# Row maxima turned by VectorE and DRAM, and stationary sides kept for a second matmul, in a transformer block on one core

## The chip, the cores and the metric

One Trainium2 chip, one of its cores. The kernel is written directly against the engines: TensorE (matmuls, PE in the profile, its weight loads PEld), VectorE (DVE), ScalarE (ACT), GpSimd (POOL) and SyncE (SP), whose queue issues nearly all DMAs. The metric is the device time of one execution in microseconds, median of several runs.

## What is computed

A block with 2048 rows of width 512: layer norm with modulation from a condition vector, attention with 32 query heads of 16 and one shared key and value head, a residual, a second modulated norm, and a gated FFN of width 1792 with another residual.

```python
mod = (_silu(c) @ w_mod).reshape(c.shape[0], 6, 1, -1)
h = _layernorm(x) * (1 + ca) + sa
q = (h @ wq) split into 32 heads of 16;  k = h @ wk;  v = h @ wv
p = softmax(q k^T * 16 ** -0.5)
x = x + ga * ((p @ v) heads joined @ wo)
h = _layernorm(x) * (1 + cb) + sb
x = x + gb * ((sigmoid(h @ w_gate) * (h @ w_up)) @ w_down)
```

The weights are scaled up, so scores are large, and the softmax needs its row maxima.

## The kernel before

Numbers are kept as pairs of fp16 (high and low part), and a product of two pairs is three matmuls: high by high, high by low, low by high (`term` gives the stationary and the moving side of the n-th of them).

**Units.** Queries are cut into 8 blocks of 256 rows and the heads into 4 groups of 8, so there are 32 units (`units`). For a unit, `qp` holds on each row half of TensorE (partitions 0 to 63 and 64 to 127) the queries of four heads: high, low and high part in 48 rows, then two rows (48 and 49) that hold minus-signed parts of the row maxima, so that a score tile comes out of the matmul with its maximum subtracted. `kp` holds the keys in the same layout.

**Two passes over the scores.** The first gives the maxima: `a_product` multiplies 128 queries of one head (stationary) with 512 keys (moving) into a bank `sa` (a ring of three), and `a_max` has VectorE reduce it to one column of `mx`. `spot(n)` tells which head, query tile and key quarter is the n-th of a unit's 64 tiles. This pass runs 84 tiles ahead (`A0`). The second pass, `st_tile`, multiplies 128 keys (stationary) with 512 query columns (moving) into a bank `st` (a ring of two), and ScalarE takes the Exp into `P`. `pv` multiplies V by `P` into the bank `craw`, in fp32, which makes two passes of each matmul.

**How maxima become rows.** When a unit's 64 tiles are done, `max_end` reduces `mx` over the key quarters (two reductions on VectorE). A step later `max_rows` has TensorE transpose the result with an identity into a bank of the `sa` ring; ScalarE scales it and rounds it to fp16; `low` has VectorE take the low part, and four DMAs on SP write the rows into `qp`.

**Small tiles.** In the main loop every product of 128 stationary columns is issued by `columns` as four matmuls of 64 rows by 32 columns, each with a weight load of its own. Products on different row halves stream at the same time.

**The main loop.** Each unit has 16 steps, each step two rounds. The order within a round is written out in `ORDER`: a0, s0, c, a1, s1 stand for the two `sa` tiles, the two `st` tiles and `pv`. The `sa` and `st` tiles of a round use one row half, `pv` the other; `sides` swaps the halves every two steps. After each round `piece` issues some terms of the projections and the FFN (the groups `pq`, `po`, `pgu`, `pd`), which a planner (`pace`, `parts`, `plan`) spreads evenly over the rounds to come; a `Couple` runs two such groups side by side, one on each row half, and swaps them at half time. `part(n0, n1)` issues the terms n0 to n1 of a couple. `piece` also calls `drip`, which issues one FFN transpose or weight load on SP. Most other follow-up work is put off by a number of steps (`defer`), so that it finds its inputs ready.

Ahead of the main loop, `PLAN` lists token by token what is issued for the first norm, the projections and the first 84 `sa` tiles. After it a tail finishes the last block with matmuls on the whole array.

Of the kernel before, what the change touches and what calls it, by code (L numbers as in the profile page):

```python
# [8 lines left out]
F16 = mybir.dt.float16  # L9
# [41 lines left out]
)  # L51
# [4 lines left out]
A0 = 84  # L56
ORDER = "a0", "s0", "c", "a1", "s1"
LAG = 2
# [38 lines left out]
def adaln_mqa_glu_kernel(  # L97
# [53 lines left out]

    def columns(dst, l_, r_, start, stop):
        for c_ in range(0, P, 32):
            pe.matmul(dst[c_:c_ + 32], l_[:, c_:c_ + 32], r_, start=start, stop=stop)

# [42 lines left out]
    class Couple:  # L198
# [3 lines left out]
        def part(self, n0, n1):  # L202
            if n0 == 0:
                for g in self.gs:
                    g.open()
            m = self.gs[0].n
            for n in range(n0, n1):
                if n == m:
                    assert self.since is not None or done[0] > self.marks
                    take_over(self.since)  # L210
                for j in (1 - side[0], side[0]):
                    g = self.gs[j ^ (n >= m)]
                    l_, r_, *cut = g.term(n % m, slice(64 * j, 64 * j + 64))
                    columns(cut[0](g.bank) if cut else g.bank, l_, r_, n == 0, n == 2 * m - 1)
                if n == m - 1:
                    self.since, self.marks = None, done[0]
                    if open_[0]:
                        hand_over()
                        self.since = done[0]
                if n in self.after:  # L220
                    self.after[n]()
            if n1 == self.n:
                for k, g in enumerate(self.gs):
                    g.end(g.bank, k == 1)
# [367 lines left out]

    def spot(n):
        return n // 16, n // 8 % 2, n % 2, n // 2 % 4

    def a_product(i, n):
# [3 lines left out]
        kc, qt, j, r = spot(n)  # L600
        sa = sbank("sa")
        l_, r_ = qp[64 * j:64 * j + 64, r, qt * P:(qt + 1) * P], kp[64 * j:64 * j + 64, kc * 512:(kc + 1) * 512]
        if first:
            pe.matmul(sa, l_, r_, start=True, stop=True)
        else:
            columns(sa, l_, r_, True, True)
        return i, n, sa

    def a_max(i, n, sa):
        kc, qt, j, r = spot(n)  # L610
# [5 lines left out]
    def a_tile(i, n):  # L616
        a_max(*a_product(i, n))

    pend, seen = [], {}

    def max_end(i):
        m16 = wp.tile([64, 32], F32, tag="m16", name="m16", bufs=4)
        for u in range(2):
            dve.tensor_reduce(m16.rearrange("p (h t u) -> p h t u", t=2, u=2)[:, :, :, u], mxs[i][64 * u:64 * u + 64],
                              axis=AX.X, op=ALU.max)
        return lambda: max_rows(i, m16)

    def max_rows(i, m16):
        qp = get_q(i)
        pm = sbank("sa")  # L630
        pe.matmul(pm[:32, :64], m16, ident[:64, :64], start=True, stop=True)
        m32 = wp.tile([32, 64], F32, tag="m32", name="m32", bufs=4)
        act.activation(m32, pm[:32, :64], AF.Identity, scale=1.0 / SM)
        mh = wp.tile([32, 2, 64], F16, tag="mh", name="mh", bufs=4)
        act.activation(mh[:, 0], m32, AF.Identity)

        def low():
            dve.tensor_tensor(mh[:, 1], m32, mh[:, 0], op=ALU.subtract)
            for h in range(2):
                for j in range(2):  # L640
                    r = 64 * j + 48 + h
                    sp1.dma_start(qp[r:r + 1], mh[16 * j:16 * j + 16, h, :])

        return low

# [193 lines left out]
    def ffn_block(b, end_of_all=False):  # L839
# [63 lines left out]
        def gu_pair(p, t, m):  # L903
# [4 lines left out]
            def term(n, rs):  # L908
                k, i = divmod(n, 3)
                h_, w_ = ((0, 0), (1, 0), (0, 1))[i]  # L910
                return h2[t][0][rs, 4 * h_ + k, :], gws[at + NDC * p + k][rs, 2 * w_ + m]
# [12 lines left out]
        def gu_last(t):  # L924
# [5 lines left out]
            def term(n, rs):  # L930
                k, i = divmod(n, 3)
                gw = gws[at + NDC * NPR + k // 2].rearrange("p m n -> p (m n)")
                h_, w_ = ((0, 0), (1, 0), (0, 1))[i]
                c0 = (2 * (k % 2) + w_) * 512
# [145 lines left out]
    def q_end(b, o):  # L1080
# [8 lines left out]
              "pm": mod_product, "me": mod_copy, "pr": mod_sum, "m": mod_end,  # L1089
              "a": a_next, "x": lambda: a_max(*held.pop(0)), "mx": lambda: rows.append(max_end(0)), "my": lambda: rows.append(rows.pop()()), "mz": lambda: rows.pop()(),  # L1090
              "lw": load_wq, "lx": load_x, "lm": lambda i: load_mod(i, sp1), "bl": lambda: blanks.append(blank(pool1)), "lq": load_q}
# [103 lines left out]
    vq = []  # L1195
    lows = []

    for i, (b, o) in enumerate(units):
# [5 lines left out]
        for kb in range(NKB):  # L1204
# [5 lines left out]
            for z in [z for z in waits if z[0] <= s]:  # L1210
                waits.remove(z)
                z[1]()
            ready_rows, rows[:] = rows[:], [max_end(*z) for z in late]
            an = A0 + 4 * (s - kb % 2)
# [3 lines left out]
            for n in range(2):  # L1218
                t = kb - kb % 2 + n
                for z in ORDER:  # L1220
                    k = int(z[1:] or 0)
                    if z[0] == "a" and an + 4 * n + 2 * k + 1 - h < len(alist):
                        a_tile(*alist[an + 4 * n + 2 * k + 1 - h])
                    if z == "c" and vq:
                        pv(*vq[n], second)
                    if z[0] == "s":
                        st_tile(i, t, k, 1 - h, second)
                if n == 0:
                    lows[:] = [z() for z in ready_rows]
                piece(s, n)  # L1230
                if n == 1:
                    for z in lows:
                        z()
            if second:
# [70 lines left out]
```

## Time and profile before

| | us |
|---|---|
| median of 3 runs | 1639.52 (1636.52 to 1640.59) |
| the profiled execution | 1629.06 |
| its span | 1627.3 |
| TensorE busy | 1585.3 (97%) |
| VectorE busy | 1417.1 (87%) |
| ScalarE busy | 1288.7 (79%) |
| first score tile of the main loop starts at | 105.1 |

A group's row gives line, engine, operation, output<-inputs, shapes and count, then busy time, mean ns of one, then the idle time before its instructions and what ended it. A timeline row gives start, length (both us), engine, line, operation and count. Nearly all instructions carry line 143, a helper that keeps the written order, so groups are told apart by the names of their tiles. Busy time of TensorE is the union of matmuls that overlap; what it could still take shows in their starts.

### The profile page before, as it was taken

The page shows a single profiled execution, that of the slowest core. Times are in us where ns is not written, and L with a number is a line of the kernel's source. Part 1 is how long each engine was busy: PE and PEld are TensorE (multiplying, and loading weights), DVE is VectorE, ACT ScalarE, POOL GpSimd, SP SyncE. Part 2 cuts the span into 40 slices and gives each one's busy share as a digit, 9 for nine tenths or more (in the row PEclk, how much of TensorE's full clock was granted, in tenths as well). Part 3 has the DMA queues.
Part 4 walks back from the last instruction along what each step waited for, and adds up shares of the span by engine and source line. Part 5 has one row for each costly group of instructions (what it writes and reads, how often), then busy time and mean ns, then how long its engine had stood idle before and what let it go on. Part 6 is the DMA issues. An engine that isn't in the chain of part 4 may idle for free.

```text
span 1627.3 us, 91846 instructions
## 1 busy us (share of the span) xinstructions
PE 1585.3 (97%) x41481; PEld 987.3 (61%) x41481; DVE 1417.1 (87%) x2400; ACT 1288.7 (79%) x2325; POOL 666.2 (41%) x827
## 2 busy tenths in 40 slices
PE   6899999999999999999999999999999999999998
PEld 3335554546666666666666666666666666665465
DVE  7789999999999999999999999999999999993041
ACT  4539998888888888888888888888888888888600
POOL 5453877244425332443226232543226322533223
PEclk9979999999999999999999999999999999999999
DMA  7122554044521233114321433115411343124411
GB/s 238 71 84 65 164 156 131 28 118 106 139 68 29 75 97 108 31 39 130 92 63 33 89 85 106 30 38 128 112 42 42 81 121 85 23 60 107 116 65 52
DMA packets 185076, 140.22 MB, mean 86 GB/s; under 512 B 96372, under 2 KB 144492, under 8 KB 184684
## 3 DMA queue, kind: packets, MB, share of 16 engines
q1 hardware_dynamic: 184684, 134.34, 30.4%
q8 instruction: 325, 5.32, 1.3%
q14 instruction: 67, 0.55, 0.1%
HBM read 97.18 MB, written 16.24 MB: 70 GB/s over the span
## 4 chain that ended last, share of the span: by engine, by line
PE 88%; DVE 4%; ACT 2%; DMA 2%; POOL 1%; issue 1%; SPq 1%; POOLq 0%; ACTq 0%; DVEq 0%
PE craw L143 24%; PE sa L143 18%; PE pgu L143 17%; PE st L143 11%; PE pd L143 8%; PE po L143 2%; PE pgu L194 2%; PE pq L143 2%; PE pd L194 2%; DVE mx L143 2%; ACT th L143 1%; DMA lc<-lD 1%; SPq L143 1%; DMA xall<-in_A_x_dram 1%; ACT P L143 1%
## 5 line engine op out<-in xcount | busy, mean ns | idle before, releaser
L143 DVE TENSOR_REDUCE mx<-sa 128x1 f32<-128x512 f32 x2048 | 1299.8, 683 | 69.6 <-PE sa L143 33.2
L143 ACT ACTIVATE P<-st 128x512 f32<-128x512 f32 x2048 | 1179.3, 598 | 204.7 <-PE st L143 143.7
L143 PE MATMUL craw<-P,V 64*32 64x512 f32 x8192 | 1086.0, 597 | 1.0 <-ACT cs L143 1.0
L143 PE MATMUL st<-qp,kp 64*32 64x512 f16 x8192 | 832.7, 379 | 7.3 <-ACT P L143 6.1
L143 PE MATMUL sa<-kp,qp 64*32 64x512 f16 (+1 forms) x7940 | 827.9, 378 | 8.2 <-DVE mx L143 6.2
L143 PEld LDWEIGHTS <-kp 64*32 64x32 f16 x8192 | 323.1, 91 | 249.2 <-issue 79.1
L143 PE MATMUL pgu<-gw,h 64*32 64x512 f16 x9408 | 407.4, 376 | 3.2 <-DMA gw<-wD 1.2
L143 PEld LDWEIGHTS <-qp 64*32 64x32 f16 (+1 forms) x7940 | 270.2, 92 | 149.1 <-issue 58.7
L143 PEld LDWEIGHTS <-h 64*32 64x32 f16 (+1 forms) x9600 | 212.7, 92 | 77.8 <-issue 22.6
L143 PEld LDWEIGHTS craw<-P,V 64*32 64x32 f32 x8192 | 184.4, 105 | 21.7 <-issue 2.6
L143 PE MATMUL pd<-wdh,g 64*32 64x512 f16 x2688 | 136.1, 376 | 0.7
L952 POOL TENSOR_SCALAR th<-th 128x512 f32<-128x512 f32 x49 | 30.2, 617 | 246.4 <-ACT th L143 223.2
L569 POOL MEMSET qp<- 32x1024 f16 x60 | 56.7, 944 | 118.6 <-PE st L143 100.5
L143 PEld LDWEIGHTS <-g 64*32 64x32 f16 x4032 | 82.0, 92 | 31.0 <-issue 6.5
L725 POOL TENSOR_TENSOR raw<-raw 128x256 f32<-128x256 f32 x31 | 22.7, 733 | 160.6 <-DMA raw<-lD 151.7
L143 PE MATMUL pd<-wdl,g 64*32 64x512 f16 x1344 | 80.5, 376 | 0.0
L953 POOL TENSOR_TENSOR th<-th,u 128x512 f32<-128x512 f32 x49 | 62.8, 1282 | 4.1
L1009 POOL TENSOR_TENSOR ot<-ot,gb 128x512 f32<-128x512 f32 x12 | 15.4, 1281 | 114.3 <-ACT ot L143 114.3
L143 DVE COPY u<-pgu 128x512 f32<-128x512 f32 (+1 forms) x49 | 31.6, 644 | 34.9 <-PE pgu L143 34.8
L143 PE MATMUL craw<-nought 64*32 64x1 f16 x357 | 58.2, 163 | 1.1 <-issue 1.1
L956 POOL TENSOR_TENSOR gr<-th,gr 128x512 f16<-128x512 f32 x49 | 57.1, 1165 | 4.1
L143 PE MATMUL pq<-h,wdh 64*32 64x512 f16 (+1 forms) x688 | 54.4, 390 | 0.1
(156 smaller groups left out, 1112.5 us busy)
## 6 DMA issues: line engine op xcount, KB each, us to landing
gw<-wD SPq DMA_DIRECT2D x224, 256.0 KB
wD<-gw SPq DMA_DIRECT2D x28, 256.0 KB
wm<-in_w_mod_dram SPq DMA_DIRECT2D x6, 1024.0 KB
qp<-qD SPq DMA_DIRECT2D x192, 32.0 KB
qD<-q SPq DMA_DIRECT2D x16, 256.0 KB
xr<-in_A_x_dram SPq DMA_DIRECT2D x16, 256.0 KB
out_dram<-ot SPq DMA_DIRECT2D x16, 256.0 KB
raw<-cs SPq DMA_DIRECT2D x248, 16.0 KB
```

What stands on the lines that cost most here:

```text
L143: return (lambda *a, **k: keep(f_(*a, **k))) if pinned else f_
L194: pe.matmul(cut[0](self.bank) if cut else self.bank, l_, r_, start=(n == 0), stop=(n == self.n - 1))
L569: eng.memset(qp[j:j + 32], 0.0)
L725: keep(pool.tensor_tensor(raw[:, :QU], raw[:, :QU], raw[:, QU:], op=ALU.mult))
L952: pool.tensor_scalar(th, th, 1.0, 1.0, op0=ALU.add, op1=ALU.mult)
L953: pool.tensor_tensor(th, th, u_, op=ALU.mult)
L956: pool.tensor_tensor(rows[:, 1], th, rows[:, 0], op=ALU.subtract)
L1009: pool.tensor_tensor(ot, ot, mods[5], op=ALU.mult)
```

## The change

Three things are changed together.

- **The maxima's way into `qp`.** `max_end` now makes one reduction over all 128 partitions and has ScalarE round its scaled result to fp16; `max_turn` has VectorE take the low part into the same tile of 32 columns and transpose that tile in blocks of 32 by 32; `max_down` writes it to DRAM in one DMA, and `max_rows` reads it back with two DMAs, each for both rows of one row half. The four parts follow one another round by round (`rows`), after the round's `piece`. TensorE has no part in it any more, and no bank of the `sa` ring.
- **Stationary sides kept.** `columns` gets `held`: with it, the four matmuls are issued without weight loads and use what the array still holds. `part` does so for the second of three terms (n % 3 == 1) unless it is the first of its piece; in `gu_pair` and `gu_last` the order of the terms is changed so that the second shares its stationary side with the first (elsewhere it did already).
- **Order of the maxima tiles.** For all units but the first, `spot` now pairs tiles: the two `sa` tiles of a round have the same head and query tile, and two neighbouring key quarters, so the second is issued as `held`. So that no other load on that row half falls between, `ORDER` becomes s0, a0, c, a1, s1.

```diff
-ORDER = "a0", "s0", "c", "a1", "s1"
+ORDER = "s0", "a0", "c", "a1", "s1"
...
-    def columns(dst, l_, r_, start, stop):
+    def columns(dst, l_, r_, start, stop, held=None):
         for c_ in range(0, P, 32):
-            pe.matmul(dst[c_:c_ + 32], l_[:, c_:c_ + 32], r_, start=start, stop=stop)
+            if held is None:
+                pe.matmul(dst[c_:c_ + 32], l_[:, c_:c_ + 32], r_, start=start, stop=stop)
+            else:
+                pe.add_instruction(mybir.InstMatmult(
+                    start_tensor_calc=start, stop_tensor_calc=stop, tile_size=(64, 32), tile_position=(held, c_), ldweights=False,
...
-                    columns(cut[0](g.bank) if cut else g.bank, l_, r_, n == 0, n == 2 * m - 1)
+                    columns(cut[0](g.bank) if cut else g.bank, l_, r_, n == 0, n == 2 * m - 1, 64 * j if n % 3 == 1 and n > n0 else None)
...
-    def spot(n):
-        return n // 16, n // 8 % 2, n % 2, n // 2 % 4
+    def spot(i, n):
+        if i == 0:
+            return n // 16, n // 8 % 2, n % 2, n // 2 % 4
+        return n // 32 * 2 + n // 2 % 2, n // 16 % 2, n % 2, n // 4 % 4
...
-            columns(sa, l_, r_, True, True)
+            columns(sa, l_, r_, True, True, 64 * j if held else None)
...
     def max_end(i):
-        m16 = wp.tile([64, 32], F32, tag="m16", name="m16", bufs=4)
-        for u in range(2):
-            dve.tensor_reduce(m16.rearrange("p (h t u) -> p h t u", t=2, u=2)[:, :, :, u], mxs[i][64 * u:64 * u + 64],
-                              axis=AX.X, op=ALU.max)
-        return lambda: max_rows(i, m16)
+        m = wp.tile([P, 16], F32, tag="m", name="m", bufs=2)
+        mm = wp.tile([P, 32], F16, tag="mm", name="mm", bufs=2)
+        dve.tensor_reduce(m, mxs[i].rearrange("p r t k -> p (r t) k"), axis=AX.X, op=ALU.max)
+        act.activation(mm[:, :16], m, AF.Identity, scale=1.0 / SM)
+        return lambda: max_turn(i, m, mm)
+
+    def max_turn(i, m, mm):
+        mt = wp.tile([P, 32], F16, tag="mt", name="mt", bufs=2)
+        mD = dr.tile([32, P], F16, tag="mD", name="mD", bufs=3)
+        dve.scalar_tensor_tensor(mm[:, 16:], m, 1.0 / SM, mm[:, :16], op0=ALU.mult, op1=ALU.subtract)
+        dve.transpose(mt, mm)
+        return lambda: max_down(i, mt, mD)
+
+    def max_down(i, mt, mD):
+        sp1.dma_start(mD.rearrange("c (b q) -> b c q", b=4), mt)
+        return lambda: max_rows(i, mD)
 
-    def max_rows(i, m16):
+    def max_rows(i, mD):
         qp = get_q(i)
-        pm = sbank("sa")
-        pe.matmul(pm[:32, :64], m16, ident[:64, :64], start=True, stop=True)
...
-            dve.tensor_tensor(mh[:, 1], m32, mh[:, 0], op=ALU.subtract)
-            for h in range(2):
-                for j in range(2):
-                    r = 64 * j + 48 + h
-                    sp1.dma_start(qp[r:r + 1], mh[16 * j:16 * j + 16, h, :])
...
+        for j in range(2):
+            r = 64 * j + 48
+            sp1.dma_start(qp[r:r + 2].rearrange("h r q -> h (r q)"), mD.rearrange("(h j r) q -> j h (r q)", h=2, j=2)[j])
...
-                h_, w_ = ((0, 0), (1, 0), (0, 1))[i]
+                h_, w_ = ((0, 0), (0, 1), (1, 0))[i]
...
-                        a_tile(*alist[an + 4 * n + 2 * k + 1 - h])
+                        a_tile(*alist[an + 4 * n + 2 * k + 1 - h], k == 1)
...
+                piece(s, n)
+                rows[:] = [z for z in [z() for z in rows] if z]
                 if n == 0:
-                    lows[:] = [z() for z in ready_rows]
-                piece(s, n)
-                if n == 1:
-                    for z in lows:
-                        z()
+                    rows.extend(max_end(*z) for z in late)
```

In `PLAN` a token `md` follows `my`, for the first unit's new `max_down`. `late` are the units whose last `sa` tile was reduced in the step before.

More of the change, by code (lines that the diff above doesn't have):

```diff
@@ L147, in adaln_mqa_glu_kernel @@
     pool1 = Ordered(nc.gpsimd)
-    def columns(dst, l_, r_, start, stop):
+    def columns(dst, l_, r_, start, stop, held=None):
         for c_ in range(0, P, 32):
-            pe.matmul(dst[c_:c_ + 32], l_[:, c_:c_ + 32], r_, start=start, stop=stop)
+            if held is None:
[3 more added lines that the diff above has]
+                    start_tensor_calc=start, stop_tensor_calc=stop, tile_size=(64, 32), tile_position=(held, c_), ldweights=False,
+                    name=nc.get_next_instruction_name(), engine=mybir.EngineType.PE,
+                    ins=[nc.tensor.lower_ap(r_), nc.tensor.lower_ap(l_[:, c_:c_ + 32])], outs=[nc.tensor.lower_ap(dst[c_:c_ + 32])]))
     turn, done, side, open_ = nc.alloc_semaphore("turn"), [0], [0], [False]
@@ L591, in sides, with a_product @@
         return (0, 1) if t // 2 % 2 == 0 else (1, 0)
-    def spot(n):
-        return n // 16, n // 8 % 2, n % 2, n // 2 % 4
-    def a_product(i, n):
+    def spot(i, n):
+        if i == 0:
+            return n // 16, n // 8 % 2, n % 2, n // 2 % 4
+        return n // 32 * 2 + n // 2 % 2, n // 16 % 2, n % 2, n // 4 % 4
+    def a_product(i, n, held=None):
         qp = get_q(i)
@@ L599, in a_product @@
             mxs[i] = wp.tile([P, 8, 2, 4], F32, tag="mx", name="mx", bufs=2)
-        kc, qt, j, r = spot(n)
+        kc, qt, j, r = spot(i, n)
         sa = sbank("sa")
@@ L605, in a_product @@
         else:
-            columns(sa, l_, r_, True, True)
+            columns(sa, l_, r_, True, True, 64 * j if held else None)
         return i, n, sa
     def a_max(i, n, sa):
-        kc, qt, j, r = spot(n)
+        kc, qt, j, r = spot(i, n)
         dve.tensor_reduce(mxs[i][:, 4 * j + r, qt, kc:kc + 1], sa, axis=AX.X, op=ALU.max)
@@ L614, in a_max, with a_tile @@
             pend.append((i,))
-    def a_tile(i, n):
-        a_max(*a_product(i, n))
+    def a_tile(i, n, held):
+        a_max(*a_product(i, n, held))
     pend, seen = [], {}
     def max_end(i):
-        m16 = wp.tile([64, 32], F32, tag="m16", name="m16", bufs=4)
-        for u in range(2):
-            dve.tensor_reduce(m16.rearrange("p (h t u) -> p h t u", t=2, u=2)[:, :, :, u], mxs[i][64 * u:64 * u + 64],
-                              axis=AX.X, op=ALU.max)
-        return lambda: max_rows(i, m16)
-    def max_rows(i, m16):
-        qp = get_q(i)
-        pm = sbank("sa")
-        pe.matmul(pm[:32, :64], m16, ident[:64, :64], start=True, stop=True)
[L632 to L637, printed above, removed]
-            dve.tensor_tensor(mh[:, 1], m32, mh[:, 0], op=ALU.subtract)
-            for h in range(2):
-                for j in range(2):
-                    r = 64 * j + 48 + h
-                    sp1.dma_start(qp[r:r + 1], mh[16 * j:16 * j + 16, h, :])
-        return low
+        m = wp.tile([P, 16], F32, tag="m", name="m", bufs=2)
[13 more added lines that the diff above has]
+    def max_rows(i, mD):
+        qp = get_q(i)
+        for j in range(2):
+            r = 64 * j + 48
+            sp1.dma_start(qp[r:r + 2].rearrange("h r q -> h (r q)"), mD.rearrange("(h j r) q -> j h (r q)", h=2, j=2)[j])
     def st_tile(i, t, pr, j, second):
@@ L932, in term @@
                 gw = gws[at + NDC * NPR + k // 2].rearrange("p m n -> p (m n)")
-                h_, w_ = ((0, 0), (1, 0), (0, 1))[i]
+                h_, w_ = ((0, 0), (0, 1), (1, 0))[i]
                 c0 = (2 * (k % 2) + w_) * 512
@@ L1089, in adaln_mqa_glu_kernel @@
               "pm": mod_product, "me": mod_copy, "pr": mod_sum, "m": mod_end,
-              "a": a_next, "x": lambda: a_max(*held.pop(0)), "mx": lambda: rows.append(max_end(0)), "my": lambda: rows.append(rows.pop()()), "mz": lambda: rows.pop()(),
+              "a": a_next, "x": lambda: a_max(*held.pop(0)), "mx": lambda: rows.append(max_end(0)), "my": lambda: rows.append(rows.pop()()), "md": lambda: rows.append(rows.pop()()), "mz": lambda: rows.pop()(),
               "lw": load_wq, "lx": load_x, "lm": lambda i: load_mod(i, sp1), "bl": lambda: blanks.append(blank(pool1)), "lq": load_q}
@@ L1195, in adaln_mqa_glu_kernel @@
     vq = []
-    lows = []
     for i, (b, o) in enumerate(units):
@@ L1212, in adaln_mqa_glu_kernel @@
                 z[1]()
-            ready_rows, rows[:] = rows[:], [max_end(*z) for z in late]
             an = A0 + 4 * (s - kb % 2)
```

18 rows, old and new, of the table PLAN are left out of this document.

## The prediction

> **What bounds the kernel now.** I read the page's first and fourth parts, then the groups of the steady stretch from 300 to 1450 us, then the timeline of TensorE by itself.
>
> ```profile
> PE 1585.3 (97%) x41481; PEld 987.3 (61%) x41481; DVE 1417.1 (87%) x2400; ACT 1288.7 (79%) x2325; POOL 666.2 (41%) x827
> PE 88%; DVE 4%; ACT 2%; DMA 2%; POOL 1%; issue 1%; SPq 1%; POOLq 0%; ACTq 0%; DVEq 0%
> ```
>
> TensorE has work in flight nearly always and carries 88% of the chain that ended last. But its busy share counts matmuls of the two row halves on top of each other. How much room is left shows only in the starts. Two rounds (a round is one pass of the inner loop: two maxima tiles `sa`, two score tiles `st`, one product `craw` with V, then a piece of FFN work `pgu`):
>
> ```profile
> 600.22 0.40 PE L143 MATMUL sa<-kp,qp 64*32 64x512 f16 x4
> 600.30 0.64 PE L143 MATMUL craw<-P,V 64*32 64x512 f32 x4
> 600.43 0.40 PE L143 MATMUL st<-qp,kp 64*32 64x512 f16 x4
> 600.65 0.40 PE L143 MATMUL sa<-kp,qp 64*32 64x512 f16 x4
> 600.76 0.61 PE L143 MATMUL craw<-P,V 64*32 64x512 f32 x4
> 600.92 0.40 PE L143 MATMUL st<-qp,kp 64*32 64x512 f16 x4
> ...
> 604.58 0.40 PE L143 MATMUL sa<-kp,qp 64*32 64x512 f16 x4
> 604.69 0.61 PE L143 MATMUL craw<-P,V 64*32 64x512 f32 x4
> 604.79 0.40 PE L143 MATMUL st<-qp,kp 64*32 64x512 f16 x4
> 605.00 0.40 PE L143 MATMUL sa<-kp,qp 64*32 64x512 f16 x4
> 605.12 0.61 PE L143 MATMUL craw<-P,V 64*32 64x512 f32 x4
> 605.22 0.40 PE L143 MATMUL st<-qp,kp 64*32 64x512 f16 x4
> 605.44 0.72 PE L143 MATMUL pgu<-gw,h 64*32 64x512 f16 x16
> 605.87 0.40 PE L143 MATMUL sa<-kp,qp 64*32 64x512 f16 x4
> ```
>
> In the second round each group of four follows the last on its row half after 0.215 us, and the two passes of `craw` on the other half after 0.43. One half takes 4 x 0.215 = 0.86, the other 2 x 0.43 = 0.86, and sixteen `pgu` matmuls (two terms on each half) 0.43: the round is 1.29 (605.87 - 604.58). In the first round the second `st` comes 0.27 after the `sa` before it, 0.055 late.
>
> ```profile
> L143 DVE TENSOR_REDUCE mx<-sa 128x1 f32<-128x512 f32 x1636 | 1043.9, 684 | 47.3 <-PE sa L143 14.3 <-PE st L143 11.6 <-PE craw L143 0.3
> L143 ACT ACTIVATE P<-st 128x512 f32<-128x512 f32 x1636 | 946.3, 598 | 160.0 <-PE st L143 112.5 <-PE sa L143 2.0
> L143 PE MATMUL craw<-P,V 64*32 64x512 f32 x6540 | 866.7, 597 | 0.3 <-ACT cs L143 0.3
> L143 PE MATMUL sa<-kp,qp 64*32 64x512 f16 x6540 | 668.2, 376 | 2.2 <-issue 1.6 <-DVE mx L143 0.6
> L143 PE MATMUL st<-qp,kp 64*32 64x512 f16 x6541 | 666.5, 377 | 2.3 <-ACT P L143 1.4 <-DMA qp<-mh 0.9
> L143 PE MATMUL pgu<-gw,h 64*32 64x512 f16 x8368 | 360.2, 376 | 2.0 <-issue 1.1 <-DMA gw<-wD 0.3
> L143 PE MATMUL pd<-wdh,g 64*32 64x512 f16 x2688 | 136.1, 376 | 0.7
> L143 PE MATMUL pd<-wdl,g 64*32 64x512 f16 x1344 | 80.5, 376 | 0.0
> L143 PE MATMUL po<-woh,a 64*32 64x512 f16 x888 | 45.5, 376 | 0.1
> L143 PE MATMUL po<-wol,a 64*32 64x512 f16 x440 | 25.6, 376 | 0.0
> L143 DVE COPY u<-pgu 128x512 f32<-128x512 f32 x37 | 25.2, 681 | 0.2 <-PE pgu L143 0.2
> L143 DVE TENSOR_REDUCE m<-mx 64x16 f32<-64x64 f32 x52 | 10.8, 207 | 0.3
> L143 DVE BATCH_NORM_STATS2 st<-xr 128x6 f32<-128x512 f32 x14 | 9.6, 684 | 0.0
> L143 DVE TENSOR_TENSOR ot<-pd,gb 128x512 f32<-128x512 f32 x12 | 8.2, 682 | 0.0
> L143 DVE TENSOR_TENSOR mh<-m,mh 32x64 f16<-32x64 f32 x26 | 5.6, 216 | 0.8
> L143 ACT ACTIVATE mh<-m 32x64 f16<-32x64 f32 x26 | 6.6, 256 | 0.8
> L143 ACT ACTIVATE m<-sa 32x64 f32<-32x64 f32 x26 | 5.1, 198 | 0.0
> L143 PE MATMUL sa<-ident,m 64*32 64x64 f32 x52 | 7.2, 217 | 0.0
> ```
>
> These 1150 us hold 1636 / 2 = 818 rounds of 1.406. The fp16 rows (6540 + 6541 + 8368 + 2688 + 1344 + 888 + 440) are 26809 matmuls; eight at a time at 0.2155 that is 722 us; `craw` is 6540 x 0.43 / 8 = 352. Streaming takes 1074 us on each half, so **76 us are gaps: 0.093 a round**. VectorE is hardly freer. Where it alone set the pace, before the loop, twenty maxima took 12.06 us, a pitch of (12.06 - 0.68) / 19 = 0.60:
>
> ```profile
> 95.72 12.06 DVE L143 TENSOR_REDUCE mx<-sa 128x1 f32<-128x512 f32 x20
> ```
>
> 1636 x 0.60 = 982, and its other rows here add some 60: 1042 of 1150. So two engines, at 93% and 91%, run through rings of three (`sa`) and two (`st`) banks; what is lost are waits between them. A change of order works on these gaps alone, and 1042 is a floor: no more than 9% could come off, and 7% by TensorE.
>
> **The change part by part.** Sums are for the 818 rounds, then times 864 / 818 for units 5 to 31 (27 x 32 rounds), where FFN work fills the loop; in units 0 to 4 TensorE has less to do.
>
> *Loads left out.* Of the `sa` groups the second of each round keeps its weights: 6540 / 4 / 2 = 817. Of FFN groups every third could (13728 / 4 / 3 = 1144), but a piece has two terms (sixteen matmuls), so about half begin a piece and load again: 570. What a load costs now:
>
> ```profile
> 600.43 0.12 PEld L143 LDWEIGHTS <-qp 64*32 64x32 f16 x4
> ```
>
> The loads for the `sa` group of 600.65 run from 600.43, where the `st` group ahead on the same half starts, to 600.55: 0.10 early. The FFN pieces above take 0.43 for two terms, which leaves no room for a load. The only exposed load is that of `craw`: its passes stand 0.46 apart at 600.30 and 0.43 at 604.69, 0.03 for four. So the bounds are 0 and, were every load so exposed, 817 x 0.03 + 570 / 2 x 0.03 = 33 us. I take a tenth of the `sa` part: **-2**. The Trainium skill ("TensorE: Matmul & The Clock Gate", What overlaps and what doesn't) has loads overlap running matmuls only where the row group differs; the rows above, same half and fully hidden, speak against it, and by it the loads would have cost far more than the 76 us of gaps that there are.
>
> *Order of a round: s0 a0 c a1 s1 in place of a0 s0 c a1 s1.* a1 and s1 stay where they are, s0 goes 0.215 earlier, a0 0.215 later. For ScalarE: an Exp can start 0.43 after its tile (0.40 in the `st` rows and 0.03) and takes 0.60. Before: s0 at 0.215, Exp 0.65 to 1.25; s1 at 0.645, ready at 1.08, Exp 1.25 to 1.85; its bank is wanted by the next s1-side tile at 0.645 + 1.29 = 1.935, so 0.08 is to spare, less what the release takes (0.05). After: Exps 0.43 to 1.03 and 1.08 to 1.68, 0.2 to spare. Over the stretch I summed how late `st` groups start behind the `sa` ahead of them (their starts, row `st` x6541): 22 us, seven tenths of it within 0.06 of the end of an Exp. The bounds are 0 and -22; I take seven tenths, 15.5, times 1.056: **-16**.
>
> For VectorE the first tile comes 0.215 later and the second at the same time. In an even round the ring holds: before, a0's bank is free at 0.43 + 0.60 + 0.13 = 1.16 and wanted by the next a1 at 0.43 + 1.29 = 1.72; after, at 1.38: 0.34 to spare in place of 0.56. But each other VectorE instruction of 0.68 (37 + 14 + 12 in the rows) pushes the maxima back 0.6, and TensorE then waits up to 0.04 before and 0.26 after. 63 x 0.22 = 14 us is the one bound, 0 the other (where VectorE ran ahead). I take half: **+7**.
>
> *Turning the maxima.* Out, for each unit: the transposition by TensorE (two matmuls of 0.22 and a bank of the `sa` ring held until ScalarE has read it), two reductions of 0.207 and one subtraction of 0.216 on VectorE, 0.198 + 0.256 on ScalarE, four row DMAs. In: one reduction (64 elements a partition, like each of the old: 0.21), one ScalarE rounding (0.2), a subtraction and a transposition on VectorE. No row shows the latter; 128x32 lies between the 0.207 of 64 elements and the 0.68 of 512; I take 0.21, so VectorE is even (0.63 and 0.63), at worst +0.47 x 27 = 13 us. The bank's gap shows in VectorE's timeline, right where the transposition stands:
>
> ```profile
> 535.35 1.98 DVE L143 TENSOR_REDUCE mx<-sa 128x1 f32<-128x512 f32 x3 [0.22 <-PE sa L143]
> ```
>
> 27 x 0.22 = **-6**. Against it a new wait: ScalarE's rounding follows the reduction within the same round, and ScalarE runs in order. It gets there after the second Exp, VectorE after the second maximum and 0.21 more; behind the rounding stand the next Exps, behind them the `st` banks. At least 0, at most a maximum and a reduction, 0.89 x 27 = 24 us; with ScalarE idle for 160.0 of 1150 us ahead of its Exps and 0.2 to spare above I take 0.2 a unit: **+5**.
>
> The rows then go through DRAM, one DMA more in the chain:
>
> ```profile
> 536.41 3.02 SPq L143 DMA_DIRECT2D qp<-mh  x4
> ...
> 542.41 0.39 PE L143 MATMUL st<-qp,kp 64*32 64x512 f16 x4
> ...
> SPq L143 <- DMA lD<-rc: 50.4, 30, 3.8
> ```
>
> The four old DMAs were issued by 539.43 and the unit's first score tile started at 542.41. The first new one can go when the turned tile is there. VectorE turns it one round ahead of the place where TensorE did, so by 535.35 above. It should land like `lD<-rc`, the same 128 pieces of 64 B (50.4 / 30 = 1.7 of waiting on SP, and 0.4 to issue, an estimate): 537.5. The two row DMAs (3.02 / 4 = 0.75 each) are out by 539.0, before the old ones. So **0**, but SP stands still for 1.7 more in each unit with the FFN's transposes and weight loads behind it; at worst one unit in four is 1.7 late, +12. The Trainium skill ("DMA: Bandwidth & Descriptors", Anatomy of one DMA) gives a DMA about 2 us of fixed cost, mostly the write's receipt; the row's 1.7 and the issue agree, and by it the sum stays.
>
> Sum: -2 - 16 + 7 - 6 + 5 = **-12 us**. The profiled execution took 1629.06 (span 1627.3 and 1.8 around it) and would take 1617. The median of the runs is 10.5 higher, so I forecast **1628** against 1639.5.
>
> **The rivals.** *A, loads count after all*: all 33 us come off besides the order's gain: 1639.5 - 33 x 1.056 - 10 = 1594 to 1605. For it: 61% of weight loading, and fewer instructions to queue. Against: the hidden loads above. *B, no change*: the gaps only move. What ScalarE no longer holds up, VectorE does, which is at 91% with one op in twenty that isn't a maximum; -16 becomes -8 and +7 stays: 1635 to 1644. *C, slower*: the pair of `sa` tiles 0.215 apart. The full 14 x 1.056 = 15 comes with a ScalarE gain of 5 only, and loads and turning cancel: 1639.5 + 10 = 1650. It decides from the point where VectorE is more than 0.34 behind when the second tile of a round is asked for. For it: three banks for two tiles that come together; against it: the `sa` row names VectorE as releaser for 0.6 us only. *D, late rows*: ScalarE's wait and the SP hop at their upper ends, 24 + 12 - 12 = +24: 1664.
>
> **How the numbers follow.** 0.3% (4.9 us) is about what can be told from no change. The forecast's case, faster by 5 to 28 us, 0.50, its own range 1616 to 1634; A 0.10; B 0.18; C 0.17; D 0.05. So faster 0.60, same 0.18, slower 0.22. The range goes from 1606 (most of A left out) to 1650 (through most of C).
>
> **What would show it.** Right: LDWEIGHTS fewer by (817 + 570) x 4 in the stretch; `st` starts at the round's head and no longer late behind `sa`; the round near 1.39; ScalarE idle ahead of one small rounding in each unit; `qp<-mD` issued some 4 us ahead of the unit's first `st`. Wrong: maxima waiting for `sa` longer than now (47.3 in the stretch), `sa` waiting for VectorE, or first tiles of a unit waiting for `qp<-mD`.

## The result, and the profile after

| | before | after |
|---|---|---|
| median | 1636.52 (7 runs, 1632.55 to 1640.59) | 1627.76 (7 runs, 1623.57 to 1631.76) |
| ratio, 95% interval | | 0.9946 [0.9931, 0.9962] |
| the profiled execution, its span | 1629.06, 1627.3 | 1623.57, 1621.8 |

A second comparison (below, `e5_after`) gave 0.9943 [0.9921, 0.9964]. The change takes off 0.54%, some 9 us of 1636; the forecast was 1628, some 11.5 less than its 1639.5. The profiled executions alone stand 5.5 apart.

The page of the kernel after, its first part:

```profile
PE 1576.0 (97%) x41417; PEld 1000.9 (62%) x41417; DVE 1415.9 (87%) x2400; ACT 1265.9 (78%) x2293; POOL 666.1 (41%) x827
```

The weight loads are all there: 41417, one for each matmul record, against 41481 before. The 64 that are gone are the loads of the old transposition (two records in each of 32 units). So one part of the change does nothing. The groups from 300 to 1450 us say the same, and show the rest:

```profile
L143 DVE TENSOR_REDUCE mx<-sa 128x1 f32<-128x512 f32 x1641 | 1044.2, 684 | 41.3 <-PE sa L143 29.6 <-PE st L143 1.8
L143 ACT ACTIVATE P<-st 128x512 f32<-128x512 f32 x1641 | 933.6, 597 | 168.9 <-PE st L143 123.2 <-PE pgu L143 2.4 <-PE sa L143 1.5
L143 PE MATMUL sa<-kp,qp 64*32 64x512 f16 x6567 | 520.3, 376 | 2.5 <-DVE mx L143 2.2 <-issue 0.2
L143 PEld LDWEIGHTS <-qp 64*32 64x32 f16 x6560 | 208.2, 92 | 67.2 <-issue 16.3
L143 PEld LDWEIGHTS <-h 64*32 64x32 f16 x8431 | 187.0, 92 | 70.2 <-issue 22.3 <-PE craw L143 1.5
L143 DVE SCALAR_TENSOR_TENSOR mm<-m,mm 128x16 f16<-128x16 f32 x26 | 9.4, 363 | 0.0
L143 ACT ACTIVATE mm<-m 128x16 f16<-128x16 f32 x26 | 5.6, 216 | 5.9 <-DVE m L143 5.0
L143 DVE STREAM_TRANSPOSE mt<-mm 128x32 f16<-128x32 f16 x26 | 5.5, 211 | 0.9
L143 DVE TENSOR_REDUCE m<-mx 128x16 f32<-128x64 f32 x26 | 5.4, 209 | 0.0
```

Every `sa` group still loads (6560 loads for 6567 matmul records). The rounds are 1641 / 2 = 820.5 in place of 818. VectorE waits less for its maxima (41.3 where 47.3 was), ScalarE a little more (168.9 for 160.0). A second profiled execution of the same kernel (`e5_after`, 1632.89) has 47.4 and 173.2, so the first of these differences is no larger than that between two executions. The reduction, the transposition (0.211) and ScalarE's rounding have the lengths that were estimated; the subtraction (`SCALAR_TENSOR_TENSOR`) has not, with 0.363 in the mean. ScalarE stands still 5.0 / 26 = 0.19 us a unit until the reduction is done.

The rows of the maxima as the trace has them, the issues of the new DMAs over the whole run:

```profile
L143 SPq DMA_DIRECT2D qp<-mD x64: 233/256/377, 97.6 to 1480.6; - x64
L143 SPq DMA_DIRECT2D mD<-mt x32: 547/610/712, 95.4 to 1478.0; - x32
```

In that view of the tile nothing is listed as having waited for it. By the trace, the issue of a unit's last row DMA ends 4.4 us (median) ahead of the unit's first score tile; before it was 3.1.

The round at the place that the prediction showed, TensorE's timeline of the kernel after:

```profile
605.03 0.61 PE L143 MATMUL craw<-P,V 64*32 64x512 f32 x4
605.07 0.38 PE L143 MATMUL st<-qp,kp 64*32 64x512 f16 x4
605.29 0.38 PE L143 MATMUL sa<-kp,qp 64*32 64x512 f16 x4
605.46 0.61 PE L143 MATMUL craw<-P,V 64*32 64x512 f32 x4
605.50 0.39 PE L143 MATMUL sa<-kp,qp 64*32 64x512 f16 x4
605.72 0.39 PE L143 MATMUL st<-qp,kp 64*32 64x512 f16 x4
```

Here the product starts level with the round's first tile, where it came 0.11 behind before, and its two passes stand 0.43 apart.

How late each kind of group starts can be summed over the stretch from the starts: start, less the start of the group before it on the same row half, less that group's streaming time (0.2157, and 0.429 for a pass of the product), us per row half. These are sums of starts, not rows of a view. `e1_order` (the new order alone, below) and the second profiled execution of the kernel after stand beside them.

| | rounds | product | its 2nd pass | `sa` | `st` | pieces | all |
|---|---|---|---|---|---|---|---|
| before (a0 s0 c a1 s1) | 817.5 | 26.0 | 6.6 | 10.1 | 11.1 | 23.0 | 76.9 |
| `e1_order` (s0 a0 c a1 s1) | 816.5 | 18.2 | 3.1 | 12.0 | 16.3 | 29.5 | 79.0 |
| after (s0 a0 c a1 s1) | 820.5 | 16.3 | 2.2 | 7.4 | 15.3 | 31.7 | 72.8 |
| `e5_after` (the same) | 817.5 | 16.9 | 2.4 | 7.2 | 17.2 | 34.6 | 78.3 |

The row half of `sa`, `st` and the product follows from `sides`. The trace does not name that of the pieces (the groups of the projections and the FFN); they were put on the half on which they fit, so a few us between pieces and the group behind a piece are uncertain. The last column goes with the execution that was profiled (the two of the kernel after took 1623.57 and 1632.89), so only the split can be compared.

The gain is not where it was looked for: with the new order the product starts sooner, the score tiles and the pieces later. The maxima tiles start sooner in the whole change only, not with the order alone.

### The profile page after: what moved, and what is told of

Same layout as the page of the kernel before. It is cut to its first block, busy times and chain, and to the rows that moved or that the text cites. A ratio compares the mean times of both kernels' runs of the same rounds, so it can differ in the third digit from the quotient of the medians.

```text
span 1621.8 us, 91775 instructions
## 1 busy us (share of the span) xinstructions
PE 1576.0 (97%) x41417; PEld 1000.9 (62%) x41417; DVE 1415.9 (87%) x2400; ACT 1265.9 (78%) x2293; POOL 666.1 (41%) x827
## 4 chain that ended last, share of the span: by engine, by line
PE 83%; DVE 6%; ACT 5%; DMA 3%; SPq 2%; issue 2%; POOL 0%; POOLq 0%; ACTq 0%; DVEq 0%
PE craw L143 22%; PE pgu L143 16%; PE sa L143 14%; PE st L143 13%; PE pd L143 7%; DVE mx L143 4%; ACT P L143 3%; PE pq L143 2%; PE pgu L200 2%; PE pd L200 2%; PE po L143 2%; SPq L143 2%; ACT th L143 1%; DMA gw<-wD 1%; DMA lc<-lD 1%
## 5 line engine op out<-in xcount | busy, mean ns | idle before, releaser
L143 ACT ACTIVATE P<-st 128x512 f32<-128x512 f32 x2048 | 1159.8, 597 | 214.9 <-PE st L143 158.8
L143 PE MATMUL sa<-kp,qp 64*32 64x512 f16 (+1 forms) x7940 | 648.2, 378 | 7.2 <-DVE mx L143 6.7
L143 PEld LDWEIGHTS <-kp 64*32 64x32 f16 x8192 | 335.4, 90 | 283.3 <-issue 113.4
L143 PE MATMUL pgu<-gw,h 64*32 64x512 f16 x9408 | 419.3, 376 | 3.9 <-DMA gw<-wD 1.3
L143 PEld LDWEIGHTS <-qp 64*32 64x32 f16 (+1 forms) x7940 | 252.9, 92 | 103.5 <-issue 45.0
L143 PEld LDWEIGHTS craw<-P,V 64*32 64x32 f32 x8192 | 237.4, 105 | 20.2 <-issue 3.2
L143 DVE COPY u<-pgu 128x512 f32<-128x512 f32 (+1 forms) x49 | 31.6, 645 | 38.4 <-PE pgu L143 38.2
L1016 POOL TENSOR_TENSOR ot<-ot,gb 128x512 f32<-128x512 f32 x12 | 15.3, 1279 | 112.3 <-ACT ot L143 112.3
```

Of the source, the lines that this page charges most:

```text
L143: return (lambda *a, **k: keep(f_(*a, **k))) if pinned else f_
L1016: pool.tensor_tensor(ot, ot, mods[5], op=ALU.mult)
```

## The experiments

Ratios are to the kernel before, run on the same chip in the same comparison.

**The parts apart.** `e1_order` is the kernel before with the new order alone, `e2_turn` with the new way of the maxima alone. The first is one line:

```diff
-ORDER = "a0", "s0", "c", "a1", "s1"
+ORDER = "s0", "a0", "c", "a1", "s1"
```

The edit of `e2_turn` is that of the change in `max_end` and behind it, with `ORDER`, `spot` and `columns` as before:

```diff
-        pm = sbank("sa")
-        pe.matmul(pm[:32, :64], m16, ident[:64, :64], start=True, stop=True)
...
+        dve.transpose(mt, mm)
...
+        sp1.dma_start(mD.rearrange("c (b q) -> b c q", b=4), mt)
```

> The kernel before with nothing but the new order of a round (s0 a0 c a1 s1); maxima turned by TensorE as before, same tiles, every weight load issued. Theory O (the order carries the gain): 0.994 to 0.997 of before, that is 5 to 9 us off, with sa waiting less for VectorE than the 31.7 us summed in the steady stretch before. Theory T (the turning of the maxima carries it): 0.999 to 1.001. Theory C (rival C of the prediction: two sa tiles 0.215 apart cost): 1.002 to 1.007.

> The kernel before with nothing but the new way of the maxima into qp (one reduction, ScalarE rounding, VectorE transposition, DRAM); old order of a round, old choice of tiles and terms. Theory O: 0.998 to 1.001 of before. Theory T: 0.994 to 0.997, with the 14th step of a unit shorter than the 2.94 us it had, and no bank of the sa ring lent. If ScalarE's wait for the reduction costs what the prediction gave it (0.2 us a unit), the step in which it stands is 0.2 longer than before (2.79 to 3.0).

Measured: order 0.9966 [0.9951, 0.9982], turning 0.9984 [0.9970, 0.9999]. Their product is 0.9950, and the whole change has 0.9946: the parts add up, and within the intervals nothing need be left for the rest of the change (the flag on the loads, the pairing of maxima tiles, the order of FFN terms), which no run has alone. By these ratios the order brings 5.6 us (2.9 to 8.0), the turning 2.6 (0.2 to 4.9).

Theory O has both times; the finer signs did not come. In `e1_order` `sa` starts no sooner in all (12.0 for 10.1 in the table above). In `e2_turn` the fourteenth step of a unit is not shorter (3.02 for 2.94), and the thirteenth, in which the rounding stands, is only 0.07 longer (2.85 for 2.79). With the new order both show: from `e1_order` to the whole change the fourteenth goes from 3.11 to 2.76 (2.83 in `e5_after`), the thirteenth from 2.79 to 3.00 (3.02). These are means of 26 units, from the starts, of one execution each.

**Loads that are really left out.** The edit that deletes loads (`e4_adjacent_noload`, below) forgets what the array holds at every matmul that has no load of its own in the list of instructions, and the fp32 product has none there. So that no product stands between the two tiles of a pair, `e3_adjacent` first moves it behind both:

```diff
-ORDER = "s0", "a0", "c", "a1", "s1"
+ORDER = "s0", "a0", "a1", "c", "s1"
```

`e4_adjacent_noload` is the same with 6544 loads deleted from the finished list of instructions (the second maxima tile of each pair, and each FFN term that has the stationary side of the term ahead of it):

```diff
+            elif load is None:
+                held.clear()
+            else:
+                at, what = tuple(z.tile_position), str(load.ins[0])
+                if held.get(at) == what and load.sync_info is None:
+                    kept.remove(load) if kept[-1] is not load else kept.pop()
+                held[at] = what
```

> The changed kernel with c moved behind the second sa tile (s0 a0 a1 c s1), every load still issued: the pair for the next run. All theories: within 0.3% of the changed kernel, 0.992 to 0.998 of before, since c runs on the other row half.

> The run before it with the weight loads really left out where the same 64x32 tile of the array already holds the same columns: 6544 of 33073 fp16 loads. Theory H (loads are hidden behind streaming): the same time as the run with loads, within 0.2%. Theory A (rival A: loads count): 1.5 to 2% less than the run with loads, that is 25 to 33 us. PEld's count falls to about 34900 in both.

(The count of loads that is given there belongs to `e4_adjacent_noload` alone; `e3_adjacent` has 41417.) Measured: 1.0123 [1.0098, 1.0149] with all loads, 1.0080 [1.0062, 1.0099] without. The page of `e4_adjacent_noload`:

```profile
PE 1606.0 (97%) x41417; PEld 907.4 (55%) x34873; DVE 1420.9 (86%) x2400; ACT 1260.5 (76%) x2293; POOL 666.1 (40%) x827
```

6544 loads out bring 1656.15 - 1648.00 = 8.2 us, 1.2 ns each: 0.43%, between what the two theories had. But none foresaw that moving the product by one place would cost 1.8%. That became the question.

**Why the product's place matters.** Two theories: the product came too late for the other row half (P), or two maxima tiles directly behind each other are too much for VectorE and the ring of three banks (V). `e6_cfirst` keeps the two tiles together and puts the product ahead of them; `e7_cfirst_noload` leaves the loads out too. `e5_after` is the changed kernel again, on the same chip.

```diff
-ORDER = "s0", "a0", "c", "a1", "s1"
+ORDER = "s0", "c", "a0", "a1", "s1"
```

> The changed kernel again, as the measure for the three that follow on the same chip. All theories: 0.993 to 0.997 of the kernel before.

> The changed kernel with the product moved ahead of both maxima tiles of its round (order s0 c a0 a1 s1); all weight loads are there. Theory P (the product's place: the run with c behind a1 lost 1.8% because the other row half was handed its work some 0.3 us late in each round): with c in second place nothing is late, so 0.990 to 0.997 of the kernel before, that is within 0.3% of the changed kernel or below it. Rival V (VectorE: two maxima tiles directly behind each other ask for two banks at once, and the ring of three has none to spare): the two tiles are just as close here, so 1.008 to 1.015, as with c behind a1.

> The same order s0 c a0 a1 s1, and 6544 weight loads really left out (second maxima tile of each pair, FFN terms with the same stationary side as the term before). If a load costs queueing wherever it stands (0.43% less for the same 6544 loads in the first comparison): 0.3 to 0.5% below the run with the same order and all loads. If the loads left out helped there only because the row halves were out of phase: within 0.15% of it.

Measured: `e5_after` 0.9943 [0.9921, 0.9964], `e6_cfirst` 1.0292 [1.0271, 1.0313], `e7_cfirst_noload` 1.0270 [1.0251, 1.0289]. P as I put it falls: with the product early the kernel is slower still. V has the sign but not the size. The loads are worth 3.8 us of 1682 here (0.23%, between the two cases of that expectation). The trace told what both theories lacked. A round of `e6_cfirst` in which VectorE and ScalarE had to wait (in the program: `st`, product, `sa`, `sa`, `st`):

```profile
603.27 0.60 PE L143 MATMUL craw<-P,V 64*32 64x512 f32 x4
603.46 0.40 PE L143 MATMUL st<-qp,kp 64*32 64x512 f16 x4
603.67 0.40 PE L143 MATMUL sa<-kp,qp 64*32 64x512 f16 x4
603.70 0.60 PE L143 MATMUL craw<-P,V 64*32 64x512 f32 x4
603.89 0.40 PE L143 MATMUL sa<-kp,qp 64*32 64x512 f16 x4
603.90 1.89 ACT L143 ACTIVATE P<-st 128x512 f32<-128x512 f32 x3 [0.57 <-PE st L143]
...
604.41 2.63 DVE L143 TENSOR_REDUCE mx<-sa 128x1 f32<-128x512 f32 x4 [0.24 <-PE sa L143]
```

The Exp starts at 603.90, 0.04 behind the end of its `st` tile. The `sa` tile ends at 604.07, but VectorE, idle from 604.17 on, starts only at 604.41: 0.11 behind the end of the product's second pass (603.70 + 0.60 = 604.30), on the other row half and in another bank. A round of `e3_adjacent`, where the program has the product behind both maxima tiles:

```profile
601.68 0.40 PE L143 MATMUL sa<-kp,qp 64*32 64x512 f16 x4
601.71 0.63 PE L143 MATMUL craw<-P,V 64*32 64x512 f32 x4
601.90 0.40 PE L143 MATMUL sa<-kp,qp 64*32 64x512 f16 x4
602.13 1.29 DVE L143 TENSOR_REDUCE mx<-sa 128x1 f32<-128x512 f32 x2 [0.49 <-PE sa L143]
602.16 0.61 PE L143 MATMUL craw<-P,V 64*32 64x512 f32 x4
602.20 0.40 PE L143 MATMUL st<-qp,kp 64*32 64x512 f16 x4
602.97 0.60 ACT L143 ACTIVATE P<-st 128x512 f32<-128x512 f32 x1 [0.33 <-PE st L143]
```

Now the maximum starts 0.05 behind its tile (602.08) while the product runs on, and it is the last `st` tile, the one behind the product in the program, whose Exp has to wait: the tile ends at 602.60, the product at 602.77, the Exp starts at 602.97. The theory that this suggests (F, for finishing in program order): a tile is handed to its reader only when all that stands ahead of it in the program has ended. Counted over the stretch, from starts and ends in the traces (reader's start less the end of the product that stands ahead of the tile in the program; in how many rounds that product ends later than the tile itself, and by how much in sum):

| tile behind the product in the program | rounds | reader's earliest start after the product's end | product ends later in | sum |
|---|---|---|---|---|
| before, a1 | 817 | +72 ns | 799 | 217 us |
| after, a1 | 820 | +70 ns | 784 | 189 us |
| `e3_adjacent`, s1 | 801 | +69 ns | 654 | 100 us |
| `e6_cfirst`, a0 | 785 | +70 ns | 785 | 315 us |

There is no exception in 3223 rounds. Readers of the first tiles ahead of the product start before it ends in most rounds (in `e3_adjacent` for a0 in 779 of 801); for a1 there it is only 144, as VectorE is busy with a0 until then. The program has no wait of that kind: one matmul of each `sa` or `st` group raises the count (a semaphore, one for all of TensorE's tiles) that its reader waits for, and of the 4096 matmuls of the product only the last of each unit raises it, for the copy out of `craw`.

That the readers were merely busy is ruled out by the times at which the count rises, which the trace has too. Behind a tile ahead of the product the first rise comes 23 to 24 ns after the tile's end in the median. Where the product ahead of a tile of the table ends over 60 ns later than the tile (2958 rounds), the count never rises between the tile's end and the product's. All this is shown for the product; groups of other kinds were not looked at.

The sums of lateness, as above, show what each place of the product costs:

| | rounds | product | its 2nd pass | `sa` | `st` | pieces | all |
|---|---|---|---|---|---|---|---|
| `e3_adjacent` (s0 a0 a1 c s1) | 801 | 41.8 | 6.3 | 4.5 | 24.0 | 23.1 | 99.7 |
| after (s0 a0 c a1 s1) | 820.5 | 16.3 | 2.2 | 7.4 | 15.3 | 31.7 | 72.8 |
| `e6_cfirst` (s0 c a0 a1 s1) | 785 | 19.7 | 2.9 | 38.6 | 12.4 | 48.4 | 122.0 |

Late in the program, the product itself starts late (41.8; so far P was right). Early, it is late by 19.7, of which 11.5 is time in which the score tile ahead of it in the program had not started either; but it holds up both maxima, and `sa` groups then start late (38.6). Of the three places the middle is best. That the holding is what costs the time in `e6_cfirst` is read from these sums.

**The product in two halves.** F has a consequence that can be tried: with half the product ahead of a tile, the tile is held for half as long. `e9_split` cuts each product into two of 256 columns (`cut`) and puts one behind each maxima tile; `e10_split_pair` keeps the maxima tiles together.

```diff
-            z = pe.matmul(c_[32 * hh:32 * hh + 32, :], V[rs, t, :], Ps[i, t, hh][rs, :], start=start, stop=stop)
+            z = pe.matmul(c_[32 * hh:32 * hh + 32, cut], V[rs, t, :], Ps[i, t, hh][rs, cut], start=start and part == 0, stop=stop and part == 1)
...
-ORDER = "s0", "a0", "c", "a1", "s1"
+ORDER = "s0", "a0", "c0", "a1", "c1", "s1"
```

The second has `"s0", "c0", "a0", "a1", "c1", "s1"` there.

> The changed kernel with the product cut into two halves of 256 moving columns each, in the order s0 a0 c' a1 c'' s1; all weight loads are there, those of the product twice. Theory F (TensorE reports its work as finished in program order across the row halves, so a1 is read by VectorE only when the product ahead of it has ended, on the other row half and in another bank): in the changed kernel the product ends later than a1 in 784 of 820 rounds of the stretch, 189 us in sum; here the part ahead of a1 ends sooner, so this sum falls below 40 us. In time little of it shows, as VectorE is busy with the maximum of a0 for most of it: 0.990 to 0.998 of the kernel before, unless the doubled fp32 loads of the product show in each round (0.024 for each of two more passes, 864 rounds): then up to 1.02. Rival V (the two maxima tiles close together and the ring of three are what costs, finishing order does not matter): no change to the changed kernel but for those loads, and a1's maximum starts as late after its matmul as before (median 446 ns).

> The same halves in the order s0 c' a0 a1 c'' s1: like the order s0 c a0 a1 s1 that cost 2.9%, but with only half the product ahead of the maxima tiles. Theory F: a0 is no longer held for 0.40 us in each round, but for 0.1 to 0.2 at most; time within 1% of the order s0 a0 c' a1 c'' s1. Rival V: the two tiles are as close as in the slow orders, so 1.02 to 1.035 of the kernel before, or more with the doubled loads.

The holding went as F says: in `e9_split` the product's part ahead of a1 ends later than a1 in 121 of 769 rounds, 9.3 us in sum (189 before the cut); in `e10_split_pair` a0 is held in 467 of 765 rounds by 0.107 in the mean, 50 us (315 in `e6_cfirst`). Again no reader starts before the product ahead of it has ended (earliest +71 and +70 ns). But a1's maximum in `e9_split` starts 440 ns behind its tile in the median, as late as in the changed kernel (446); V had said so, and F had allowed for it, since VectorE is still busy with a0. In time both lost far more than either theory allowed: 1.0451 [1.0416, 1.0487] and 1.0475 [1.0450, 1.0501]. They are within 1% of each other, as F had it, but V's bound for the second ("more with the doubled loads") is met too, so the times decide nothing. Groups from 300 to 1450 us of `e9_split`:

```profile
L143 PE MATMUL craw<-P,V 64*32 64x256 f32 x12316 | 869.8, 379 | 13.6 <-issue 12.7
L143 PEld LDWEIGHTS craw<-P,V 64*32 64x32 f32 x12312 | 400.4, 106 | 89.0 <-issue 36.4 <-ACT cs L143 1.2 <-PE craw L143 0.5
```

Twice the fp32 loads, 400 us of them for 200 after. The lateness of all groups is 141.4 per half in place of 72.8, of which the product's own groups have 32 more; where the other 37 come from was not settled. So no run shows what the holding alone is worth in time.

**The wait of ScalarE.** `e8_late_round` issues the rounding one round behind the reduction:

```diff
-        act.activation(mm[:, :16], m, AF.Identity, scale=1.0 / SM)
-        return lambda: max_turn(i, m, mm)
+        def rounded():
+            act.activation(mm[:, :16], m, AF.Identity, scale=1.0 / SM)
+            return lambda: max_turn(i, m, mm)
+        return rounded() if i == 0 else rounded
```

> The changed kernel, with ScalarE's rounding of the maxima issued one round behind VectorE's reduction in place of the same round (units 1 to 31), so that ScalarE doesn't wait for it; the rest of the chain follows one round later each. If the wait costs what the sum said (+5 us): 0.2 to 0.4% below the changed kernel. Rival (ScalarE has the time to spare, the wait costs nothing): within 0.1% of it. If the rows then come late: 0.3% above it or more, with first score tiles waiting for qp<-mD.

Measured: 0.9930 [0.9911, 0.9949], against 0.9943 for the changed kernel on the same chip: 0.13% less, between the two expectations, and the intervals overlap. The trace has both sides of it:

```profile
L143 PE MATMUL st<-qp,kp 64*32 64x512 f16 x6568 | 673.2, 377 | 5.4 <-DMA qp<-mD 3.4 <-ACT P L143 0.8
L143 ACT ACTIVATE mm<-m 128x16 f16<-128x16 f32 x26 | 5.4, 209 | 0.0
```

The wait ahead of the rounding is gone (5.9 to 0.0), and the step of a unit in which it stood, the thirteenth of sixteen, takes 2.77 where it took 3.00 (means of 26 units, from the starts). But the last step takes 3.01 where it took 2.78: the rows are issued a round later, 2.9 us ahead of the first score tile in the median, and three of the four units of the stretch that have only 1.1 to 1.2 us wait 3.4 us for them together.

**FFN loads alone, and both edits.** With the order as it is, only the FFN's loads can be left out; `e11_ffn_noload` deletes them in the same way (2632 loads). `e12_both` does so too and has the late rounding, with the write to DRAM moved up into the round of the turning:

```diff
-        return lambda: max_down(i, mt, mD)
+        return max_down(i, mt, mD) if i else lambda: max_down(i, mt, mD)
```

> The changed kernel with the 2632 weight loads of FFN terms really left out (a term with the same stationary side as the term before on the same row half in the same piece); order and all else as in the changed kernel, the maxima tiles keep their loads. By the gain of 0.43% for 6544 loads in the first comparison and 0.22% in the second: 0.1 to 0.2% below the changed kernel, 0.992 to 0.994 of the kernel before. If FFN loads are hidden entirely (two terms stream in 0.43 us in the trace): within 0.05% of the changed kernel. If loads count after all: 0.8% below it.

> The changed kernel with the two edits that each came out a little below it: the 2632 FFN weight loads really left out, and ScalarE's rounding of the maxima one round behind the reduction; the write to DRAM now follows the turning in the same round, so that the rows are issued no later than in the changed kernel. If both gains are real and add (0.13% and 0.3% by the medians, and the three first score tiles that waited 3.4 us for late rows no longer do): 0.988 to 0.991 of the kernel before. If they were scatter: 0.993 to 0.996, like the changed kernel itself.

Measured: `e11_ffn_noload` 0.9911 [0.9891, 0.9932], `e12_both` 0.9891 [0.9869, 0.9912]. The first is 0.3% below the changed kernel by the ratios, more than the 0.1 to 0.2% expected, but the intervals overlap, and its own runs span 0.5%; the second lies clear of the changed kernel's 0.9946 [0.9931, 0.9962] and beats both kernels, with 1618.74 (1614.56 to 1621.57) against 1636.21 before. Its page and its groups:

```profile
PE 1569.9 (97%) x41417; PEld 961.5 (59%) x38785; DVE 1410.1 (87%) x2400; ACT 1266.0 (78%) x2293; POOL 667.6 (41%) x827
```

```profile
L143 PE MATMUL st<-qp,kp 64*32 64x512 f16 x6588 | 674.7, 377 | 4.8 <-issue 3.1 <-ACT P L143 0.4
L143 ACT ACTIVATE mm<-m 128x16 f16<-128x16 f32 x26 | 5.5, 210 | 0.0
```

This is what was expected if both gains are real (0.988 to 0.991). 41417 - 38785 = 2632 loads are gone, ScalarE doesn't wait, the row of `st` names no wait for `qp<-mD`, and the thirteenth and the last step take 2.76 and 2.79. The stretch has 6588 / 8 = 823.5 rounds.

## Why the prediction came out as it did

The total held: 11.5 us foretold, 9 measured. Term by term it was partly luck: one part had no effect to price, other terms have the wrong size or sign, and the errors cancel in part. The round of the profiled execution came to 1150 / 820.5 = 1.402, not "near 1.39".

- **Loads left out (-2).** They were not left out. The flag on the matmul changed nothing: the profile counts a load for every matmul, so "LDWEIGHTS fewer by (817 + 570) x 4", the first thing that was to show the step right, shows it wrong. That a part of the change might not do what it says was no rival of mine here, and the diff alone did not let one see it. The size was near all the same, since the term was small: 6544 loads really left out are worth 8.2 us in one order and 3.8 in the other, so 5548 would be some 3 to 7 (an estimate in proportion; by the unsure 5 us of `e11_ffn_noload` for 2632 loads, some 11). Rival A (33 us) falls by this, not merely by the kernel after. The reading behind it stands: a load hidden beside the running matmul of its own row half costs next to nothing.
- **Order, -16 and +7.** The net, -9, lies just outside the 2.9 to 8.0 us that `e1_order` gains. The terms do not hold one by one. With the order alone `st` got later, not sooner (11.1 to 16.3); `sa` got later as the +7 had it, but by little (10.1 to 12.0); and the product, which had no term at all, gained most (26.0 to 18.2). The 22 us of which the -16 was taken are also the sum over both row halves; counted per half, as the 76 us of gaps are, they are 11. I had taken each row half for itself and each tile as ready when its own streaming ends. Since a1 and s1 wait for the product ahead of them in the program, what counts is when the product starts relative to them; in the timelines above it moved from 0.11 behind the round's head to level with it. The sum by which the product outlasts a1 fell from 217 to 189, and for s1 from 44 to 33. That the gained time comes from this is argued, not shown: a1's maximum starts 446 ns behind its tile in the median, 398 before. "`st` no longer late behind `sa`" came true in words only, as it now stands first and bears what the round begins late with. Why the product itself starts sooner in the new order, though two tiles stand ahead of it in both, no run tells apart.
- **Turning, -6 and +5.** Net -1; `e2_turn` has -2.6 (0.2 to 4.9). The +5 was the right mechanism, and in the new order the right size: 0.19 us a unit of ScalarE's standing still, the thirteenth step 0.21 longer than in `e1_order`, and 0.23 shorter again in `e8_late_round`. The -6 was 0.22 a unit at the fourteenth step, which falls by 0.28 to 0.35 in the new order. In the old order the first does not show and the second hardly (`e2_turn` above), so the two parts of the change are not independent step by step, although their times add up. The transposition took 0.211 where 0.21 was guessed, the subtraction 0.363 in the mean where 0.216 was taken over from the old one; so VectorE was not even, but had some 0.15 a unit more.
- **Rows through DRAM, 0.** Right: nothing waits for `qp<-mD`, and it leaves 4.4 us ahead of the first score tile, where "some 4" was foretold. SP waits 1.36 us for each write (`DMA mD<-mt`: 38.2 us in 28 waits) where 1.7 was taken, and issues one in 0.61 where 0.4 was. That the slack is real shows when it is spent: in `e8_late_round` three of the units that are left with 1.2 us or less wait.
- **Rivals.** C (the pair of tiles 0.215 apart) did not come: `sa` waits for VectorE for 2.2 us, where 0.6 was (0.7 in `e5_after`), and the maxima for `sa` no longer than before in all (41.3 and 47.4 for 47.3). Its "more than 0.34 behind" can matter in few rounds of this order. In `e6_cfirst`, where the product holds both maxima up, something like it does: 38.6 us of lateness of `sa` per half. Of B (no change, the gaps only move) the words fit the split of the lateness better than the forecast did; its mechanism, that VectorE then holds things up, and its sum do not. D (late rows) fell.

## What to carry to other kernels

When work for two row halves is interleaved in one program, look for each tile at what stands ahead of it in the program, on either half: in these kernels no reader got a tile before the long product ahead of it had ended. Try such a matmul behind the tiles that are waited for, but early enough that its own half isn't idle; here one place forward cost 3.5%, one place back 1.8%. A profile is of one execution: compare two of the same kernel before a difference of a few us is read from it. And when a change says that it removes instructions, count them in the profile first: the rest of the explanation depends on it.

## What the runs showed of the hardware

- **Finishing is told in program order, across row halves.** In 3223 rounds of four kernels no reader starts before the product ahead of its tile has ended (earliest +69 ns), and in the 2958 of them in which the product ends clearly later than the tile, TensorE's count does not rise in between, though tile and product share neither row half nor bank. Starting is another matter: in the kernel after, the product starts before the `sa` tile just ahead of it in the program in 762 of 820 rounds, by 190 ns in the median. The Trainium skill ("TensorE: Matmul & The Clock Gate", What overlaps and what doesn't) has matmuls both start and end strictly in program order. The runs agree on the end, as far as the readers tell it, and differ on the start.
- **A load on the same row half can be free, nearly.** 6544 loads of 64 rows by 32 columns were worth 1.2 ns each in one order and 0.6 in the other, where a load takes 92 ns (`LDWEIGHTS <-qp`, above).
- **Cutting the fp32 product in two costs dearly.** The same streaming in passes of 256 columns, with twice the loads, made the kernel 5% slower than the changed one (1.0451 / 0.9946).
